# Sigmoid attention with a mixture-of-depths block: picking the routed rows on VectorE instead of on TensorE

## The chip, the cores and the metric

The kernel runs on one core of one Trainium2 chip. A core has five engines that each work through a list of instructions of their own in program order: TensorE (PE, matmuls), VectorE (DVE), ScalarE (ACT), GpSimd (POOL) and SyncE (SP, which here only issues transfers). Data moves between DRAM and the on-chip memory by DMA. The metric is the device time of one execution in microseconds (us); lower is better.

## The reference

Two blocks follow one another. All arrays are float32.

```python
# q, k, v: (8, 12, 448, 64)
scores = scale * np.matmul(q, k.transpose(0, 1, 3, 2)) - np.log(S)
attn = 1.0 / (1.0 + np.exp(-scores))
attn_out = np.matmul(attn, v)
x = attn_out.transpose(0, 2, 1, 3).reshape(8, 448, 768)
# w_gate: (768,), w1: (768, 1024), w2: (1024, 768), capacity: 128
scores = np.einsum('bsd,d->bs', x, w_gate)
out = x.copy()
for b in range(B):
    top_idx = np.argpartition(-scores[b], capacity)[:capacity]
    xe = x[b, top_idx]
    ye = np.maximum(xe @ w1, 0.0) @ w2
    g = 1.0 / (1.0 + np.exp(-scores[b, top_idx]))
    out[b, top_idx] = x[b, top_idx] + g[:, None] * ye
```

So every sequence b has 448 tokens; the 128 with the highest gate score are "routed": they go through a two-layer network, and the others are copied.

## The kernel before

**Steps and pieces.** Four heads of one sequence form a group; there are 24 groups, taken in pairs: 12 *steps* s (`stream`, L463). A step has seven *units* n = 0..6 (`unit`, L193): 32 matmuls make scores into two PSUM tiles named `psc` (of which there are two in all), and two ACT instructions (L220) turn them into `attn`. I write u(s,n) for a unit. Between the units `gap(s, n)` (L445) places other work: in gaps 0 to 2, and in the last gap of the step before, the product with v (`values`, L226, 48 or 64 matmuls into the two PSUM tiles `o`); in gaps 3 to 5 one piece of the routed network (`go`, L406). A gap may take a second piece in n = 5.

**The way of one sequence.** When the last of its three groups has gone through `values`, `take` (L259) transposes the result on DVE into `x_b`, `store` (L280) sends it to a DRAM tile `x_d` by four DMAs on SP, and `gate_part`/`gate` (L269, L290) compute the scores on DVE. `spread` (L300) copies the scores to all partitions with a matmul (L304), ACT makes `rep` of it (L307), and DVE puts each token's own score into `tok_gate` (L309, L313). `rank` (L316), four times, counts for each token the tokens above it, with two DVE instructions each (L321, L324). `place` (L328) adds the counts to a rank and compares it with 0..127 into a matrix of zeros and ones, `sel` (L333). `select` (L336) multiplies this matrix with (token number, score): eight small matmuls (L340) that leave the numbers and the scores of the routed tokens in PSUM, in columns of a `psc` tile that the unit does not use. `fetch` (L343) makes row numbers of them on DVE (L345, L347), the sigmoid of the score on ACT (L349), and an indirect DMA on POOL (L351) gathers the rows as `xe`. `turn_rows` (L356) transposes `xe` with six matmuls (L361). The network then has six pieces for a sequence: three of `ffn1` (L377, 36, 36 and 24 matmuls: g0, g1, g2) and three of `ffn2` (L386, 16 matmuls each: p0, p1, p2), each with an ACT or DVE instruction behind it.

**Where these stand.** `routed(b)` (L421) writes the order out by hand: `late` holds what is placed in gap (s, n), `beside` what is placed inside unit (s, n), between its matmuls and its first ACT instruction. For sequence 0 (called the first sequence; its s is 2): spread in gap (2,5), ranks and place in (2,6), select and fetch inside u(3,1), turn_rows and g0 in (3,3). For sequences 1 to 5 select stands inside u(s+1,0), turn_rows in gap (s+1,3). For sequences 6 and 7 `choose` (L496) places select and fetch behind the last unit. Between the select of sequence 7 and its turn_rows three pieces of sequence 6 are left for PE.

**Loads.** `load(i)` (L90) brings k and q of a group, `turn(i)` (L175) transposes them on DVE; there are two raw buffers of each, so load(i+2) waits for turn(i). `load_v(s+1)` (L100) stands at the start of step s, and its buffer is that of step s-1, read until `values(s-1, 3)` in gap (s,2). `load_weights` (L123) follows it in the steps 1, 2 and 3: five, five and four of the 14 tiles of w1 and w2. All of these, store and `copy_out` (L287) are issued by SP in program order.

Of the kernel before, what the change touches and what calls it, by code (L numbers as in the profile page):

```python
# [17 lines left out]
def kernel(  # L18
# [11 lines left out]
    nc = tc.nc  # L30
# [69 lines left out]
    def load_v(s):  # L100
# [15 lines left out]
        for n in range(4):  # L116
            nc.sync.dma_start(out=th[n * TT:(n + 1) * TT],
                              in_=blocks(4 * (n // 2), HK + n % 2, 4, 1))

    w1_sb = const.tile([P, KD, F], F32, name="w1_sb")  # L120
    w2_sb = const.tile([P, KF, D], F32, name="w2_sb")

    def load_weights(n0, n1):  # L123
        for n in range(max(n0, 0), min(n1, KD + KF)):
            if n < KD:
                nc.sync.dma_start(out=w1_sb[:, n], in_=moe_w1[n * P:(n + 1) * P, :])
            else:
                m = n - KD
                nc.sync.dma_start(out=w2_sb[:, m], in_=moe_w2[m * P:(m + 1) * P, :])
# [6 lines left out]
    wg_b = const.tile([P, HP, TT], F32, name="wg_b")  # L136

    earlier = const.tile([P, NC, S], mybir.dt.uint8, name="earlier")
    iota_r = const.tile([P, CAP], F32, name="iota_r")

    tok_gate = [const.tile([P, NC, 2], F32, name=f"tok_gate{n}") for n in range(2)]
    above = const.tile([P, NC], F32, name="above")
    level = const.tile([P, NC], F32, name="level")
    sel = const.tile([P, NC, CAP], F32, name="sel")

    def constants():
        nc.gpsimd.memset(ones, 1.0)
        make_identity(nc, iden)
        for a in range(4):
            p = slice(a * TT, (a + 1) * TT)  # L150
            nc.gpsimd.dma_start(
                out=wg_b[p],
                in_=bass.AP(tensor=moe_w_gate.tensor, offset=moe_w_gate.offset + a * TT,
                            ap=[[0, TT], [P, HP], [1, TT]]))
        nc.gpsimd.iota(iota_r, pattern=[[1, CAP]], base=0, channel_multiplier=0,
                       allow_small_or_imprecise_dtypes=True)
        for t in (above, level):
            nc.gpsimd.memset(t, 0.0)
        for t in tok_gate:
            nc.gpsimd.memset(t, 0.0)  # L160
            for a in range(4):
                nc.gpsimd.iota(t[a * TT:(a + 1) * TT, :, 0], pattern=[[4, NC]], base=a,
                               channel_multiplier=TB, allow_small_or_imprecise_dtypes=True)
        number = moe.tile([P, TB, TT], F32, name="rep")
        nc.gpsimd.iota(number, pattern=[[1, TB], [TB, TT]], base=0, channel_multiplier=0,
                       allow_small_or_imprecise_dtypes=True)
        for c in range(NC):
            nc.gpsimd.tensor_scalar(
                out=earlier[:, c, :], in0=number.rearrange("p r t -> p (r t)"),
                scalar1=tok_gate[0][:, c, 0:1], scalar2=None, op0=ALU.is_lt)  # L170


    qT, kT, attn, outs = {}, {}, {}, {}
# [19 lines left out]
    def unit(s, n):  # L193


        if (s == 0 and n in (1, 3, 5)) or (s in (1, 2) and n == NF + 1):
            psc = [banks(0), banks(1)]
        else:
            psc = [banks("psc"), banks("psc")]
        if n == NF:  # L200
            parts = [(x, HK) for x in range(2)]
        else:
            x, c = divmod(n, NF + 1)
            parts = [(x, 4 * c), (x, 4 * c + 2)]
        for e in range(2):
            for y, (x, r) in enumerate(parts):
                for h in range(4):
                    d = slice(h * TT, (h + 1) * TT)
                    nc.tensor.matmul(  # L209
                        psc[h // 2][y * Dh:(y + 1) * Dh, h % 2, :S],  # L210
                        kT[2 * s + x][d, e, r:r + 2, :].rearrange("d r t -> d (r t)"),
                        qT[2 * s + x][d, e].rearrange("d r t -> d (r t)"),
                        start=(e == 0), stop=(e == 1))
        more = beside.pop((s, n), [])
        for fn, args in more:
            fn(*args, psc[0][:, 0, S:])
        for pr in range(2):
            a = attnp.tile([P, 2, S], F32, name=f"attn{pr}", bufs=NU + 3)
            attn[s, pr, n] = a
            nc.scalar.activation(a, psc[pr][:, :, :S], AF.Sigmoid, bias=bias_s, scale=QK_SCALE)  # L220
            if pr == 0:
                for fn, args in more:
                    fetch(*args, psc[0][:, 0, S:])

    x_tiles, gate_parts, st = {}, {}, {}
    def values(s, n):  # L226
# [72 lines left out]

    def spread(b, where="o"):  # L300

        tg = tok_gate[b % 2]
        ps = banks(where)[:, 0, :S]
        nc.tensor.matmul(ps, ones, st[b].pop("diag").rearrange("p r t -> p (r t)"),  # L304
                         start=True, stop=True)
        rep = moe.tile([P, S], F32, name="rep")
        nc.scalar.activation(rep, ps, AF.Copy)  # L307
        rep_t = moe.tile([P, TB, TT], F32, name="scr")
        nc.vector.transpose(rep_t, ps.rearrange("p (r t) -> p r t", t=TT))  # L309
        for a in range(4):  # L310
            p = slice(a * TT, (a + 1) * TT)
            n = len(range(a, TB, 4))
            nc.vector.tensor_copy(tg[p, :n, 1], rep_t[p, a:TB:4, 0])  # L313
        st[b]["rep"] = rep

    def rank(b, c):  # L316
        tg, rep = tok_gate[b % 2], st[b]["rep"]
        n = P if c < NC - 1 else LAST
        own = tg[:n, c, 1:2]
        junk = moe.tile([P, S], F32, name="scr")  # L320
        nc.vector.tensor_scalar(out=junk[:n], in0=rep[:n], scalar1=own, scalar2=0.0,  # L321
                                op0=ALU.is_gt, op1=ALU.add, accum_out=above[:n, c:c + 1])
# [3 lines left out]
            op0=ALU.is_equal, op1=ALU.mult, accum_out=level[:n, c:c + 1])  # L326

    def place(b):  # L328
        pl = moe.tile([P, NC], F32, name="place")
        nc.vector.tensor_add(pl, above, level)  # L330
        for c in range(NC):
            n = P if c < NC - 1 else LAST
            nc.vector.tensor_scalar(out=sel[:n, c], in0=iota_r[:n], scalar1=pl[:n, c:c + 1],  # L333
                                    scalar2=None, op0=ALU.is_equal)

    def select(b, s0, n, pk):  # L336

        tg = tok_gate[b % 2]
        for c in range(NC):
            nc.tensor.matmul(pk[:n, 0:2], sel[:, c, s0:s0 + n], tg[:, c, :],  # L340
                             start=(c == 0), stop=(c == NC - 1))

    def fetch(b, s0, n, pk):  # L343
        row = moe.tile([P, 1], I32, name="row", bufs=2)
        nc.vector.tensor_copy(row[:n], pk[:n, 0:1])  # L345
        idx = moe.tile([P, 1], I32, name="idx", bufs=2)
        nc.vector.tensor_scalar_add(idx[:n], pk[:n, 0:1], float(b * S))  # L347
        gt = moe.tile([P, 1], F32, name="gate", bufs=2)
        nc.scalar.activation(gt[:n], pk[:n, 1:2], AF.Sigmoid)  # L349
        xe = moe.tile([P, D], F32, name="xe", bufs=2)  # L350
        nc.gpsimd.indirect_dma_start(  # L351
            out=xe[:n], out_offset=None, in_=st[b]["x_d"][:, :],
# [56 lines left out]
            fn(*args, where)  # L409

    late = {}
    beside = {}

    def put(where, s, n, fn, *args):
        where.setdefault((s, n), []).append((fn, args))
# [5 lines left out]
    def routed(b):  # L421

        s = (NG * b + NG - 1) // 2 + 1
        put(late, s, 5 if b == 0 else 4, spread, b)
        for c in range(NC - 1):
            put(late, s, 6 if b == 0 else 4, rank, b, c)
        put(late, s, 6, rank, b, NC - 1)
        put(late, s, 6, place, b)
        if s == NS:
            return  # L430
        put(late, *((s + 1, 1) if b == 0 else (s, 6)), copy_out, b)
        for s0, n in SLOTS:
            if s + 1 < NS:
                put(beside, s + 1, 1 if b == 0 else 0, select, b, s0, n)
            put(late, s + 1, 3, turn_rows, b, n)
            put(late, s + 1, 3, routed_groups, b, n)

    def gates(i):
        gate_part(i)
# [5 lines left out]
    def gap(s, n):  # L445
# [11 lines left out]
        if n == NU - 1 and s < NS:  # L457
            values(s, 0)
        due(late, s, n)
        if n == 3 and s > 0:  # L460
            gates(2 * s - 1)

    def stream():  # L463
# [1 line left out]
            routed(b)  # L465
        load(0)
        load(1)
        nc.vector.memset(sel, 0.0)
        nc.vector.memset(bias_s, NEG_LOG_S)
        turn(0)  # L470
        load(2)
        load_v(0)
        warm = banks(1)
        for _ in range(3):
            nc.tensor.matmul(warm[:, 0], sel[:, 0, :], sel.rearrange("p c n -> p (c n)"),  # L475
                             start=True, stop=True)
        constants()
        for s in range(NS):
            for n in range(NU):
# [3 lines left out]
                    load(2 * s + 3)  # L483
                if n == 0:
                    load_v(s + 1)
                    load_weights(5 * s - 5, 5 * s)
                if s == 0 and n == 1:
                    nc.vector.tensor_reduce(
                        out=iden_t, in_=iden.rearrange("p (a t) -> p t a", t=TT),
                        axis=AX.X, op=ALU.add)  # L490
                gap(s, n)
                if n == NU - 2:
                    turn(2 * s + 2)
                    load(2 * s + 4)

        def choose(b):  # L496
            for s0, n in SLOTS:
                pk = banks("psc")[:, 0]
                select(b, s0, n, pk)
                fetch(b, s0, n, pk)  # L500

        choose(B - 2)
        for n in range(5):
            gap(NS, n)
        for n in range(3):
            go("any")
        due(late, NS, NU - 1)
        choose(B - 1)
        copy_out(B - 1)
        while len(ready) > 1:  # L510
            go("any")
        for s0, n in SLOTS:
# [1 line left out]
            routed_groups(B - 1, n)  # L514
        while ready:
            go("any")
        assert not late and not beside

    with tc.manual_schedule():
        stream()  # L520
# [29 lines left out]
```

## Time and profile before

| | |
|---|---|
| median of 3 runs | 488.0 us (488.0 to 489.94) |
| the profiled execution | 489.37 us, its span 487.6 us |
| PE busy in the span | 470.9 us (97%) |
| DVE, ACT, POOL busy | 211.7, 189.4 and 28.0 us |
| mean granted TensorE clock | 0.988 |
| DRAM read and written | 53.58 and 25.17 MB |

The span runs from the first to the last instruction of the profiled execution; its time is 1.8 us longer. PE is busy nearly all the time, so a moment in which PE is idle, or a matmul that is not needed, is time of the kernel, while DVE and ACT have room on average. The clock is the share of full TensorE speed that the hardware granted; it is 1.00 in nearly every stretch of this execution.

### The profile page before, as it was taken

To read this page: it belongs to the slowest core of one execution; us is meant where nothing else is said; L and a number is where in the kernel's file an instruction comes from. 1 tells how busy PE (TensorE), PEld (TensorE's weight loads), DVE (VectorE), ACT (ScalarE), POOL (GpSimd) and SP (SyncE) were. 2 spreads that over 40 slices of the span, in tenths; PEclk is the share of its full clock that TensorE was granted. 3 is DMA by queue.
4 is the path that set the end of the run, shared out by engine and by line. 5 is a ranking of instruction groups with operands and counts; after the bars stand their busy time and mean duration, and the time that the engine had idled before them with its cause. 6 is when DMAs were issued, how large, how long until landed. Compare 5 with 4: busy or idle time off the path is not lost.

```text
span 487.6 us, 14593 instructions
## 1 busy us (share of the span) xinstructions
PE 470.9 (97%) x6662; PEld 309.5 (63%) x6662; DVE 211.7 (43%) x461; ACT 189.4 (39%) x253; POOL 28.0 (6%) x45
## 2 busy tenths in 40 slices
PE   8998999499999999999999999999999999999995
PEld 3554646386568465577567476568576667489994
DVE  4315296508252168268152156456433355184101
ACT  4746464223442453544352552543343445011010
POOL 8000000000000000010000000010000000001000
PEclk9999999789999999999999999999999999999999
DMA  8929298985463078498262075658632036165000
GB/s 264 198 83 336 107 311 137 304 249 104 176 152 109 3 166 155 169 221 202 99 153 99 13 173 95 223 131 167 214 82 82 35 59 172 34 97 182 14 34 32
DMA packets 117277, 68.67 MB, mean 141 GB/s; under 512 B 95648, under 2 KB 108000, under 8 KB 116960
## 3 DMA queue, kind: packets, MB, share of 16 engines
q1 hardware_dynamic: 115808, 61.35, 49.0%
q0 software_dynamic: 1408, 6.39, 4.3%
q8 instruction: 52, 0.85, 0.7%
q14 instruction: 9, 0.07, 0.0%
HBM read 53.58 MB, written 25.17 MB: 161 GB/s over the span
## 4 chain that ended last, share of the span: by engine, by line
PE 85%; issue 4%; DMA 3%; DVE 3%; SPq 2%; ACT 1%; POOLq 0%; DVEq 0%; ACTq 0%
PE o L250 24%; PE psc L209 24%; PE o L377 16%; PE o L386 13%; SPq L285 2%; PE o L209 2%; DMA x_d<-x_b 1%; PE psc L386 1%; DMA xe<-x_d,row 1%; PE psc L340 1%; PE o L304 1%; PE o L361 1%; PE o L475 1%; DVE x_b L265 1%; PE psc L377 1%
## 5 line engine op out<-in xcount | busy, mean ns | idle before, releaser
L220 ACT ACTIVATE attn<-psc,bias_s 128x896 f32<-128x896 f32 x158 | 151.1, 1003 | 130.6 <-PE psc L209 117.3
L209 PE MATMUL psc<-qT,kT 32*64 32x448 f32 x2528 | 150.3, 540 | 1.9 <-ACT attn L220 1.9
L250 PE MATMUL o<-attn,raw_v 32*64 32x448 f32 x2304 | 134.7, 536 | 0.7 <-ACT o L253 0.7
L209 PEld LDWEIGHTS psc<-qT,kT 32*64 32x64 f32 x2528 | 61.5, 131 | 61.1 <-issue 37.4
L250 PEld LDWEIGHTS o<-attn,raw_v 32*64 32x64 f32 x2304 | 60.3, 132 | 48.6 <-issue 38.8
L377 PEld LDWEIGHTS o<-xeT,w_sb 128*128 128x128 f32 x672 | 78.9, 197 | 10.7 <-issue 7.9
L377 PE MATMUL o<-xeT,w_sb 128*128 128x128 f32 x672 | 81.7, 282 | 0.9 <-ACT xeT L367 0.9
L386 PE MATMUL o<-w_sb,hT 128*128 128x256 f32 x320 | 73.4, 383 | 0.0
L265 DVE STREAM_TRANSPOSE x_b<-o 128x448 f32<-128x448 f32 x48 | 26.9, 618 | 106.9 <-PE o L250 83.7
L386 PEld LDWEIGHTS o<-w_sb,hT 128*128 128x128 f32 x320 | 59.4, 190 | 16.8 <-issue 5.8
L184 DVE STREAM_TRANSPOSE kT<-raw_k 128x384 f32<-128x384 f32 x48 | 24.7, 554 | 30.2 <-DMA raw_k<-in_k_dram 15.0
L388 DVE SCALAR_TENSOR_TENSOR xe<-o,gate,xe 128x256 f32<-128x256 f32 x20 | 9.7, 483 | 51.5 <-PE o L386 51.5
L379 ACT ACTIVATE hT<-o 128x384 f32<-128x384 f32 (+1 forms) x21 | 9.5, 454 | 56.9 <-PE o L377 56.9
L278 DVE TENSOR_REDUCE gate_p<-scr 128x14 f32<-128x896 f32 x24 | 26.1, 1087 | 0.8
L250 PE MATMUL o<-attn,raw_h 32*64 32x448 f32 x384 | 26.4, 534 | 0.0
L272 DVE TENSOR_TENSOR scr<-x_b,wg_b 128x896 f32<-128x896 f32 x24 | 25.6, 1067 | 0.1
L191 DVE STREAM_TRANSPOSE qT<-raw_q 128x896 f32<-128x896 f32 x23 | 24.7, 1074 | 1.9 <-DMA raw_q<-in_q_dram 1.9
L351 POOL DMA_INDIRECT xe<-x_d,row x8 | 7.9, 987 | 297.0 <-DVE idx L347 222.8
L324 DVE SCALAR_TENSOR_TENSOR scr<-rep,tok_gate,earlier 128x448 f32<-128x448 f32 (+1 forms) x32 | 21.8, 683 | 1.1
L321 DVE TENSOR_SCALAR_CACHE_REDUCE scr<-rep,tok_gate 128x448 f32<-128x448 f32 (+1 forms) x32 | 21.4, 669 | 0.9
L309 DVE STREAM_TRANSPOSE scr<-o 128x448 f32<-128x448 f32 x8 | 5.2, 650 | 37.6 <-ACT rep L307 37.6
L253 ACT ACTIVATE o<-bias_s 1x1 f32<-1x1 f32 x36 | 5.9, 165 | 36.8 <-PE o L250 24.9
(56 smaller groups left out, 204.7 us busy)
## 6 DMA issues: line engine op xcount, KB each, us to landing
raw_k<-in_k_dram SPq DMA_DIRECT2D x24, 448.0 KB, 4.6
raw_q<-in_q_dram SPq DMA_DIRECT2D x24, 448.0 KB, 4.5
x_d<-x_b SPq DMA_DIRECT2D x32, 336.0 KB, 6.7
out_dram<-x_d SPq DMA_DIRECT2D x8, 1344.0 KB, 9.0
raw_v<-in_v_dram SPq DMA_DIRECT2D x48, 192.0 KB, 3.9
w_sb<-in_moe_w_dram SPq DMA_DIRECT2D x6, 512.0 KB, 6.1
w_sb<-in_moe_w_dram SPq DMA_DIRECT2D x8, 384.0 KB, 5.2
raw_h<-in_v_dram SPq DMA_DIRECT2D x48, 32.0 KB, 5.5
```

The source lines that it names most:

```text
L184: nc.vector.transpose(kT[i][:, e, :HK], sk[:, e, :HK].rearrange("p (m c) d -> p c m d", c=NF))
L191: nc.vector.transpose(qT[i], sq)
L209: nc.tensor.matmul(psc[h // 2][y * Dh:(y + 1) * Dh, h % 2, :S], kT[2 * s + x][d, e, r:r + 2, :].rearrange("d r t -> d (r t)"), qT[2 * s + ...
L220: nc.scalar.activation(a, psc[pr][:, :, :S], AF.Sigmoid, bias=bias_s, scale=QK_SCALE)
L250: nc.tensor.matmul(o[x][j * Dh:(j + 1) * Dh, pr, :S], w, a[rows, j, :], start=(n == 0 and c == 0), stop=(n == 3 and c == NF - 1))
L265: nc.vector.transpose(x_tiles[b][:, :, 2 * g + pr, :], outs[s][x][:, pr, :S].rearrange("p (r t) -> p r t", t=TT))
L272: nc.vector.tensor_tensor(out=tmp, in0=x_tiles[b][:, :, 2 * g:2 * g + 2, :].rearrange("p r h d -> p r (h d)"), in1=wg_b[:, 2 * g:2 * g + 2 ...
L278: nc.vector.tensor_reduce(out=gate_parts[b][:, :, g], in_=tmp, axis=AX.X, op=ALU.add)
L321: nc.vector.tensor_scalar(out=junk[:n], in0=rep[:n], scalar1=own, scalar2=0.0, op0=ALU.is_gt, op1=ALU.add, accum_out=above[:n, c:c + 1])
L324: nc.vector.scalar_tensor_tensor(out=junk[:n], in0=rep[:n], scalar=own, in1=earlier[:n, c, :], op0=ALU.is_equal, op1=ALU.mult, accum_out=l ...
L377: nc.tensor.matmul(ps[:, f - f0, :n], w1_sb[:, t, f * P:(f + 1) * P], xeT[:, t, :n], start=(t == 0), stop=(t == KD - 1))
L386: nc.tensor.matmul(ps[:n, :ND], st[b]["hT"][:, t, :n], w2_sb[:, t, cols], start=(t == 0), stop=(t == KF - 1))
```

## The change

The selection matmuls, `sel`, `iota_r` and `beside` go. `place` writes the 448 ranks to a DRAM tile `ranks` by a DMA on SP and reads them back by a second one, broadcast to all partitions (`spot`). `select` compares `spot` with the partition's own number on DVE and sums token numbers (int16) and scores where it is equal: two DVE instructions. It stands in gap (s+1,0) for every sequence but the last. All four ranks and place stand in the gap of spread. The weights are loaded at four points instead of three. For the first sequence turn_rows and g0 move from gap (3,3) to (3,4); in step 2 `turn(6)` and `load(8)` move from n = 5 to n = 3, and the gate of group 3 from n = 3 to n = 6.

```diff
+    WEIGHTS = {(1, 0): (0, 3), (1, NU - 2): (3, 9), (2, 0): (9, 11), (3, 1): (11, KD + KF)}
...
     def place(b):
         pl = moe.tile([P, NC], F32, name="place")
         nc.vector.tensor_add(pl, above, level)
-        for c in range(NC):
-            n = P if c < NC - 1 else LAST
-            nc.vector.tensor_scalar(out=sel[:n, c], in0=iota_r[:n], scalar1=pl[:n, c:c + 1],
-                                    scalar2=None, op0=ALU.is_equal)
-
-    def select(b, s0, n, pk):
-        tg = tok_gate[b % 2]
-        for c in range(NC):
-            nc.tensor.matmul(pk[:n, 0:2], sel[:, c, s0:s0 + n], tg[:, c, :],
-                             start=(c == 0), stop=(c == NC - 1))
-
-    def fetch(b, s0, n, pk):
+        ranks = dram.tile([NC, P], F32, name="ranks")
+        nc.sync.dma_start(out=ranks.rearrange("c p -> p c"), in_=pl)
+        spot = moe.tile([P, S], F32, name="spot")
+        nc.sync.dma_start(out=spot, in_=bass.AP(tensor=ranks.tensor, offset=ranks.offset,
+                                                ap=[[0, P], [1, S]]))
+        st[b]["spot"] = spot
+
+    def select(b, s0, n):
+        picked = []
+        for what in (number.rearrange("p r t -> p (r t)"), st[b]["rep"]):
+            got = moe.tile([P, 1], F32, name="got", bufs=4)
+            junk = moe.tile([P, S], F32, name="scr")
+            nc.vector.scalar_tensor_tensor(
+                out=junk[:n], in0=st[b]["spot"][:n], scalar=slots[s0][:n], in1=what[:n],
+                op0=ALU.is_equal, op1=ALU.mult, accum_out=got[:n, 0:1])
+            picked.append(got)
         row = moe.tile([P, 1], I32, name="row", bufs=2)
-        nc.vector.tensor_copy(row[:n], pk[:n, 0:1])
+        nc.vector.tensor_copy(row[:n], picked[0][:n])
         idx = moe.tile([P, 1], I32, name="idx", bufs=2)
-        nc.vector.tensor_scalar_add(idx[:n], pk[:n, 0:1], float(b * S))
+        nc.vector.tensor_scalar_add(idx[:n], picked[0][:n], float(b * S))
         gt = moe.tile([P, 1], F32, name="gate", bufs=2)
-        nc.scalar.activation(gt[:n], pk[:n, 1:2], AF.Sigmoid)
+        nc.scalar.activation(gt[:n], picked[1][:n], AF.Sigmoid)
...
         put(late, s, 5 if b == 0 else 4, spread, b)
-        for c in range(NC - 1):
-            put(late, s, 6 if b == 0 else 4, rank, b, c)
-        put(late, s, 6, rank, b, NC - 1)
-        put(late, s, 6, place, b)
+        for c in range(NC):
+            put(late, s, 5 if b == 0 else 4, rank, b, c)
+        put(late, s, 5 if b == 0 else 4, place, b)
         if s == NS:
             return
         put(late, *((s + 1, 1) if b == 0 else (s, 6)), copy_out, b)
         for s0, n in SLOTS:
-            if s + 1 < NS:
-                put(beside, s + 1, 1 if b == 0 else 0, select, b, s0, n)
-            put(late, s + 1, 3, turn_rows, b, n)
-            put(late, s + 1, 3, routed_groups, b, n)
+            put(late, s + 1, 0, select, b, s0, n)
+            put(late, s + 1, 4 if b == 0 else 3, turn_rows, b, n)
+            put(late, s + 1, 4 if b == 0 else 3, routed_groups, b, n)
...
-        if n == 3 and s > 0:
+        if n == (NU - 1 if s == 2 else 3) and s > 0:
             gates(2 * s - 1)
...
                 if n == 0:
                     load_v(s + 1)
-                    load_weights(5 * s - 5, 5 * s)
...
                 gap(s, n)
-                if n == NU - 2:
+                if n == (NF if s == 2 else NU - 2):
                     turn(2 * s + 2)
                     load(2 * s + 4)
+                load_weights(*WEIGHTS.get((s, n), (0, 0)))
...
-        choose(B - 2)
         for n in range(5):
             gap(NS, n)
         for n in range(3):
             go("any")
-        due(late, NS, NU - 1)
-        choose(B - 1)
         copy_out(B - 1)
+        for s0, n in SLOTS:
+            select(B - 1, s0, n)
```

Here NU is 7, NF is 3 and NC is 4. The constants change to match: a `slots` tile with the partition's number, `number` with the token numbers as int16 (made on POOL), and `above` starts at 448, so that the 64 unused places of `ranks` equal no slot.

More of the change, by code (lines that the diff above doesn't have):

```diff
@@ L123, in load_weights @@
     def load_weights(n0, n1):
-        for n in range(max(n0, 0), min(n1, KD + KF)):
+        for n in range(n0, n1):
             if n < KD:
@@ L138 @@
     earlier = const.tile([P, NC, S], mybir.dt.uint8, name="earlier")
-    iota_r = const.tile([P, CAP], F32, name="iota_r")
-    tok_gate = [const.tile([P, NC, 2], F32, name=f"tok_gate{n}") for n in range(2)]
+    number = const.tile([P, TB, TT], mybir.dt.int16, name="number")
+    slots = {s0: const.tile([P, 1], F32, name=f"slot{s0}") for s0, _ in SLOTS}
+    score = const.tile([P, NC], F32, name="score")
     above = const.tile([P, NC], F32, name="above")
     level = const.tile([P, NC], F32, name="level")
-    sel = const.tile([P, NC, CAP], F32, name="sel")
     def constants():
@@ L154, in constants @@
                             ap=[[0, TT], [P, HP], [1, TT]]))
-        nc.gpsimd.iota(iota_r, pattern=[[1, CAP]], base=0, channel_multiplier=0,
-                       allow_small_or_imprecise_dtypes=True)
[L157 to L166, printed above, removed]
+        for s0, slot in slots.items():
+            nc.gpsimd.iota(slot, pattern=[[0, 1]], base=s0, channel_multiplier=1,
+                           allow_small_or_imprecise_dtypes=True)
+        nc.gpsimd.memset(above, float(S))
+        nc.gpsimd.memset(level, 0.0)
+        nc.gpsimd.memset(score, 0.0)
+        mine = moe.tile([P, NC], F32, name="place")
+        for a in range(4):
+            nc.gpsimd.iota(mine[a * TT:(a + 1) * TT], pattern=[[4, NC]], base=a,
+                           channel_multiplier=TB, allow_small_or_imprecise_dtypes=True)
+        every = moe.tile([P, TB, TT], F32, name="rep")
+        nc.gpsimd.iota(every, pattern=[[1, TB], [TB, TT]], base=0, channel_multiplier=0,
+                       allow_small_or_imprecise_dtypes=True)
+        nc.gpsimd.tensor_copy(number, every)
         for c in range(NC):
             nc.gpsimd.tensor_scalar(
-                out=earlier[:, c, :], in0=number.rearrange("p r t -> p (r t)"),
-                scalar1=tok_gate[0][:, c, 0:1], scalar2=None, op0=ALU.is_lt)
+                out=earlier[:, c, :], in0=every.rearrange("p r t -> p (r t)"),
+                scalar1=mine[:, c:c + 1], scalar2=None, op0=ALU.is_lt)
     qT, kT, attn, outs = {}, {}, {}, {}
@@ L213, in unit @@
                         start=(e == 0), stop=(e == 1))
-        more = beside.pop((s, n), [])
-        for fn, args in more:
-            fn(*args, psc[0][:, 0, S:])
         for pr in range(2):
@@ L220, in unit @@
             nc.scalar.activation(a, psc[pr][:, :, :S], AF.Sigmoid, bias=bias_s, scale=QK_SCALE)
-            if pr == 0:
-                for fn, args in more:
-                    fetch(*args, psc[0][:, 0, S:])
     x_tiles, gate_parts, st = {}, {}, {}
@@ L312, in spread @@
             n = len(range(a, TB, 4))
-            nc.vector.tensor_copy(tg[p, :n, 1], rep_t[p, a:TB:4, 0])
+            nc.vector.tensor_copy(score[p, :n], rep_t[p, a:TB:4, 0])
         st[b]["rep"] = rep
     def rank(b, c):
-        tg, rep = tok_gate[b % 2], st[b]["rep"]
+        rep = st[b]["rep"]
         n = P if c < NC - 1 else LAST
-        own = tg[:n, c, 1:2]
+        own = score[:n, c:c + 1]
         junk = moe.tile([P, S], F32, name="scr")
@@ L330, in place @@
         nc.vector.tensor_add(pl, above, level)
-        for c in range(NC):
-            n = P if c < NC - 1 else LAST
-            nc.vector.tensor_scalar(out=sel[:n, c], in0=iota_r[:n], scalar1=pl[:n, c:c + 1],
-                                    scalar2=None, op0=ALU.is_equal)
-    def select(b, s0, n, pk):
-        tg = tok_gate[b % 2]
-        for c in range(NC):
-            nc.tensor.matmul(pk[:n, 0:2], sel[:, c, s0:s0 + n], tg[:, c, :],
-                             start=(c == 0), stop=(c == NC - 1))
-    def fetch(b, s0, n, pk):
+        ranks = dram.tile([NC, P], F32, name="ranks")
[13 more added lines that the diff above has]
+            picked.append(got)
         row = moe.tile([P, 1], I32, name="row", bufs=2)
-        nc.vector.tensor_copy(row[:n], pk[:n, 0:1])
+        nc.vector.tensor_copy(row[:n], picked[0][:n])
         idx = moe.tile([P, 1], I32, name="idx", bufs=2)
-        nc.vector.tensor_scalar_add(idx[:n], pk[:n, 0:1], float(b * S))
+        nc.vector.tensor_scalar_add(idx[:n], picked[0][:n], float(b * S))
         gt = moe.tile([P, 1], F32, name="gate", bufs=2)
-        nc.scalar.activation(gt[:n], pk[:n, 1:2], AF.Sigmoid)
+        nc.scalar.activation(gt[:n], picked[1][:n], AF.Sigmoid)
         xe = moe.tile([P, D], F32, name="xe", bufs=2)
@@ L411 @@
     late = {}
-    beside = {}
     def put(where, s, n, fn, *args):
@@ L467, in stream @@
         load(1)
-        nc.vector.memset(sel, 0.0)
+        zero = moe.tile([P, 512], F32, name="scr")
+        nc.vector.memset(zero, 0.0)
         nc.vector.memset(bias_s, NEG_LOG_S)
@@ L474, in stream @@
         for _ in range(3):
-            nc.tensor.matmul(warm[:, 0], sel[:, 0, :], sel.rearrange("p c n -> p (c n)"),
-                             start=True, stop=True)
+            nc.tensor.matmul(warm[:, 0], zero[:, :P], zero, start=True, stop=True)
         constants()
@@ L491, in stream @@
                 gap(s, n)
-                if n == NU - 2:
+                if n == (NF if s == 2 else NU - 2):
                     turn(2 * s + 2)
                     load(2 * s + 4)
[L496 to L500, printed above, removed]
-        choose(B - 2)
+                load_weights(*WEIGHTS.get((s, n), (0, 0)))
         for n in range(5):
@@ L516, in stream @@
             go("any")
-        assert not late and not beside
+        assert not late
     with tc.manual_schedule():
```

## The prediction

> **What bounds the kernel now.** I read the engines' busy times first: PE is busy 470.9 of 487.6 us, so I count what PE is given and where it stands still. The chain of waits confirms it, except in one place, the first routed sequence (its lines: start, length, what):
>
> ```profile
> 78.53 7.14 DMA x_d<-x_b
> 86.54 6.74 DMA xe<-x_d,row
> 93.42 1.53 PE o L361 x6
> 95.83 6.62 PE o L377 x36
> 104.14 4.21 PE o L377 x36
> ```
>
> PE waits for the gathered rows, which wait for the store of x. The windows by stage give PE 2.20 us of work between 87 and 96: 6.8 us idle. The same 36 matmuls take 6.62 us here and 4.21 later, because the granted clock (before "DMA share" in this view) fell:
>
> ```profile
> 94.00:96.00 2.00, 1.10 (x6) 0.70 (x5) 0.00 (x0) 0.81 (x1) 0.00 (x0) 0.50 1.04 382
> 98.00:100.00 2.00, 2.00 (x11) 2.00 (x11) 0.00 (x0) 0.00 (x0) 0.00 (x0) 0.50 1.59 652
> 101.00:102.00 1.00, 1.00 (x12) 1.00 (x11) 0.00 (x0) 0.00 (x0) 0.00 (x0) 1.00 1.58 667
> ```
>
> The stall costs 6.8 + 2.4 = 9.2 us. Next, the timeline of PE at u(6,0), with a select, and at u(5,0), without one:
>
> ```profile
> 193.28 1.71 PE L209 MATMUL psc<-qT,kT 32*64 32x448 f32 x32
> 194.92 1.05 PE L340 MATMUL psc<-tok_gate,sel 128*128 128x2 f32 x8
> 195.91 1.76 PE L250 MATMUL o<-attn,raw_v 32*64 32x448 f32 x32
> 198.96 1.71 PE L209 MATMUL psc<-qT,kT 32*64 32x448 f32 x32
> ...
> 160.68 1.71 PE L209 MATMUL psc<-qT,kT 32*64 32x448 f32 x32
> 165.19 1.71 PE L209 MATMUL psc<-qT,kT 32*64 32x448 f32 x32
> ```
>
> Unit to unit is 5.68 us with, 4.51 without: a select costs PE 1.17 us. Last, SP's own queue around the first store:
>
> ```profile
> 59.87 1.81 SPq L115 DMA_DIRECT2D raw_v<-in_v_dram  x4
> 67.77 13.41 SPq L285 DMA_DIRECT2D x_d<-x_b  x4
> 81.70 2.17 SPq L96 DMA_DIRECT2D raw_k<-in_k_dram  x1
> 83.97 0.37 SPq L96 DMA_DIRECT2D raw_q<-in_q_dram  x1
> ```
>
> The queue stands until `values(1,3)` frees the v buffer (59.87), then issues v, five weights, k, q, and is held by the store for 13.41 us; load(8) follows.
>
> **1. Selects removed from PE.** Sequences 1 to 5: 5 x 1.17 = 5.85 us. Sequence 6: its matmuls start at 415.90, the next ones at 416.89: 1.0. Sequence 7: 0.8 (446.26 to 447.05). Together **-7.65**. Sequence 0's lies inside the stage counted in 2.
>
> **2. The first sequence.** When can `spot` be there? SP: three weights fewer in front (512 + 2 x 384 KB = 1.31 MB). Transfers were saturated there (333 to 392 GB/s between 66 and 74), so the store's data moves 3.5 us forward. In the before trace it ran from 74 to 85, and SP was free at 81.2; after, 70.5 to 81.5 and 77.6. Behind it stands load(8), k and q, 2.6 us: the ranks' write is issued at 80.6. DVE has them by 75.6 (copies end 69.6, four ranks at 1.45, the add 0.16), so the added write waits for SP, not SP for it. Its data waits for k and q (0.92 MB at 390 GB/s, until 83.8) and lands at about 85; the read needs 2.6 us: a 448 KB load on a quiet queue (near 118) lands after 3.2, of which 1.15 are its bytes, and `spot` has 0.55 us of bytes. **Spot at 87.8.** Neither transfer has a row. Bounds: quiet legs of 2.05 and 2.6 without any queueing, 85.3; the gather's 6.7 at this place and raw_h's median of 5.5, 92.8. I take 87.8, built from the rows of this queue.
>
> The page "DMA: Bandwidth & Descriptors" of the Trainium skill (Specifications) speaks against the write: pieces below 512 B are not moved at line rate but by read-modify-write. The nearest row is the store with 2688 pieces of 128 B in 2.70 us, 1.0 ns each; the 512 pieces of 4 B then take 0.5 us, which is in my 85. If the rule doubled that, the sum would be 0.5 us worse here and 0.5 at the end.
>
> What is queued behind it? On DVE, select stands in gap (3,0): two sums at 0.77 (L324's 0.69 and 0.08), then turn(7), 2.4 us. On ACT, the sigmoid of select stands **ahead of the activations of u(3,1)**. Before, that sigmoid waited 0.29 us. Now it waits for spot; u(3,2) needs the psc tiles that those activations read. u(3,2) would start at 80.4. Now: sigmoid at 87.8 + 1.6, first activation done 1.1 later, 90.5, second 91.5. PE stands still for 10 us and runs at half clock after it: in the trace of before the clock fell 3.2 us into the idle time and came back 4.8 us after work went on without a break. From spot on: u(3,2) goes on at +3.7; it and values(2,3), 3.7 us of work, end at +9.9; take 2.3, gate 2.2, gate 2.2 + 0.8 on DVE, +17.4; spread(1), which now stands ahead of g0, +18.3; g0 and, to be level with the trace before, g1: 8.4, **+26.7 = 114.5**. The trace before has the same work done at 109.1 (start of u(3,5)). Loss **+5.4**, which includes the select that is gone. Bounds by those of spot: +2.9 and +10.4. The stall of 87 to 96 does go; a longer one replaces it, 7 us earlier. The gather, issued at 90, has landed by 97 (6.7) and is hidden by u(3,3).
>
> "TensorE: Matmul & The Clock Gate" of the skill (Part 1) gives some 3.4 us of sustained work until full speed. The 4.8 us of this trace disagree. By the page the sum would be 0.7 us lower.
>
> **3. Sequences 1 to 6.** Spot is two quiet legs, 5.2 us, behind the ranks and the store. Tightest is sequence 2: ranks end at 191.4, the store's data at about 193; spot 198, first activation done 200.7. u(6,2) starts at 202.93 - 1.17 = 201.8, and one more piece, 3.65 us, now stands between, as the first sequence's pieces are one gap behind. So 0, with 4.7 us of cover. The same count gives 3 (sequence 1) and about 5 (3, 4, 5). Sequence 6: ranks at 414.5, spot 419.7, gather landed by 427 against turn_rows at 429.4 - 1.0. 0, cover 1.4. DVE does not grow: select's 1.5 us stand against the four compares' 1.1.
>
> **4. The end.** Sequence 7: ranks 442.7, spot 448.2, gather issued 450.1, 5.4 us as before: 455.5. PE is at turn_rows at 456.75 - 0.8 = 455.9. With 0.5 us for the small pieces it just misses: **+0.4** (0 to +6, with 5.5 us a leg).
>
> **5. At nothing.** The four ranks in one gap: between spread and the next use of the `o` tiles PE has 10 us, DVE 9. The constants: POOL is idle from 12.4 on, first need at 70. Weights 3 to 8 at (1,5): transfers at 3 GB/s between 55 and 60, so they fit ahead of v; without that room the store would be 3 us later, and so the stall longer. turn(6), load(8), gate 3: DVE has the room; load(8) ahead of the ranks' write is in 2.
>
> Sum: -7.65 + 5.4 + 0.4 = **-1.85**. From the span of 487.6 that is 485.75, from this execution's 489.37, 487.5; the median is 1.4 us below that execution: **486.1**.
>
> **The rivals.** *Spot comes early.* If the write passed the k and q in front of it and SP were not held by the store, spot could come before 82: then stage 2 breaks even, and at 78 (turn_rows no longer waits) the whole 9.2 + 1.17 come back. For it: DVE is done at 75.6. Against it: 13.41 us of store in SP's queue. Midway: -7.65 - 5 + 0 = **475.4**. Chance 0.26.
>
> *The round trip decides, slower.* Each us more on it costs one us at the first sequence and one at the end, from 3 us on sequence 1 too, from 1.4 sequence 6. It turns the sum past +0.5% at 2.2 us more than mine. With legs of 5.5 (raw_h's median), at 4 us more: -7.65 + 9.4 + 4.4 + 1 + 2.6 = +9.8, **497.8**. For it: the 4 B pieces have no row; against: queues are quiet at the end (30 to 180 GB/s). Chance 0.15.
>
> *It does not do what it says.* The 1.17 us a sequence don't come back, because ACT, with the sigmoid in front, paces the units instead: then 0 in 1, and with 5.4 + 0.4, **493.8**. Against: ACT is busy 189.4 of 487.6. Chance 0.05.
>
> **How the numbers follow.** The forecast has 0.54, its own range 483 to 491. A measurement of this kernel can tell about 0.5% (2.4 us) from nothing: below 485.6 is faster, above 490.4 slower. Of the forecast's 0.54, 0.21 fall below, 0.30 between, 0.03 above. With the early spot faster has 0.47; same 0.30 and a little from the round trip at 1 to 2 us more, 0.32; slower 0.21. The range goes from the early rival's near side to the first us of the late one: 476 to 493.
>
> **What would show it.** L340 gone from PE, and u(s,0) to u(s,1) at 4.5 us throughout. In step 3 PE idle before u(3,2) from about 80, released by ACT, which waits for select; the ranks' write issued near 80.6 and spot near 88; half clock until about 97. No idle PE in the later steps, and less than 1 us before the last turn_rows. Wrong: an unbroken PE between 80 and 92 (early rival), or idle PE ahead of u(s+1,2) in several steps (late rival).

## The result and the profile after

The changed kernel takes 543.4 us (four executions, 540.9 to 543.7) against 488.5 for the kernel before: a ratio of 1.111, 95% interval 1.107 to 1.115. The forecast was 486.1, its range 476 to 493. The span of the profiled execution grew from 487.6 to 541.6 us. These lines of the page after (engines; the clock granted, in tenths over 40 slices; the groups of instructions) answer to those of before:

```profile
span 541.6 us, 14483 instructions
...
PE 481.4 (89%) x6598; PEld 312.1 (58%) x6598; DVE 215.9 (40%) x461; ACT 189.1 (35%) x253; POOL 27.7 (5%) x41
...
PEclk9999996799899999999999999899999999699799
...
L214 PE MATMUL psc<-qT,kT 32*64 32x448 f32 x2528 | 164.9, 554 | 35.7 <-ACT attn L222 34.0
...
L343 DVE SCALAR_TENSOR_TENSOR scr<-spot,slot,number 128x448 f32<-128x448 f32 x8 | 5.5, 685 | 112.5 <-DMA spot<-ranks 112.5
...
L352 ACT ACTIVATE gate<-got 128x1 f32<-128x1 f32 x8 | 1.6, 203 | 67.4 <-DVE scr L343 67.4
```

PE was idle 16.7 us before and is idle 60.2 now, and although 64 matmuls are gone (8.3 us busy before) it is busy 10.5 us longer, in part because the clock falls in the long waits. The windows by stage around four of the waits (the clock stands before the last two columns, DMA share and GB/s) show it below 1.00 in three of them, and at 1.00 in a shorter one, near 388:

```profile
78.00:98.80 20.80, 3.29 (x72) 1.68 (x56) 2.73 (x11) 1.18 (x3) 0.86 (x1) 0.68 0.34 79
137.00:146.60 9.60, 2.51 (x58) 0.95 (x43) 2.63 (x10) 1.22 (x3) 0.91 (x1) 0.85 0.69 215
...
386.00:391.00 5.00, 2.50 (x46) 1.44 (x35) 2.77 (x10) 1.34 (x3) 0.57 (x1) 1.00 0.97 399
457.00:466.00 9.00, 1.75 (x21) 0.74 (x25) 1.51 (x6) 0.37 (x2) 0.00 (x0) 0.73 0.60 178
```

The score matmuls (L214) waited 34.0 us for ACT; the first instruction of select (L343) waited 112.5 us for `spot`, and the sigmoid behind it on ACT (L352) 67.4 us for select. The chain is plain in the kernel's step s = 3. First SP's queue, with start and length of each issue:

```profile
81.86 0.39 SPq L331 DMA_DIRECT2D ranks<-place  x1
...
93.09 0.33 SPq L333 DMA_DIRECT2D spot<-ranks  x1
```

The read can be issued only when the write has landed: 11.2 us. Then DVE, ACT and PE, each a timeline (start, length, engine, line; in brackets the idle time before it and what ended it):

```profile
96.16 0.69 DVE L343 SCALAR_TENSOR_TENSOR scr<-spot,slot,number 128x448 f32<-128x448 f32 x1 [18.04 <-DMA spot<-ranks]
```

```profile
97.62 0.20 ACT L352 ACTIVATE gate<-got 128x1 f32<-128x1 f32 x1 [19.82 <-DVE scr L343]
...
97.73 1.89 ACT L222 ACTIVATE attn<-psc,bias_s 128x896 f32<-128x896 f32 x2
```

```profile
78.80 2.46 PE L249 MATMUL o<-attn,raw_v 32*64 32x448 f32 x46
98.77 3.43 PE L214 MATMUL psc<-qT,kT 32*64 32x448 f32 x26 [17.51 <-ACT attn L222]
```

The sigmoid of select stands ahead of the activations of u(3,1); u(3,2) needs the psc tiles that they read. So a transfer of 2 KB stops PE for 17.5 us, by way of three engines (SP, DVE and ACT). The same happens at each later sequence: 7.1 us at sequence 1, 1.6 to 2.5 at 2, 4 and 5, 0.5 at 3, 7.0 at 6, 7.5 at 7. And the DMA engines were not busy meanwhile. The windows after the ranks' write of sequence 6, which was issued at 449.41:

```profile
450.00:451.00 1.00, 0.67 (x16) 0.00 (x0) 0.00 (x0) 0.16 (x1) 0.00 (x0) 1.00 0.32 18
451.00:452.00 1.00, 0.94 (x24) 0.55 (x32) 0.00 (x0) 0.01 (x1) 0.00 (x0) 1.00 0.03 0
...
457.00:458.00 1.00, 0.72 (x9) 0.41 (x9) 0.00 (x0) 0.00 (x0) 0.00 (x0) 1.00 0.00 0
```

Its packets are over by 452; it lands at 457.9. Sequence 2, whose write meets a quiet queue too, shows both legs, the write and the read:

```profile
209.29 0.39 SPq L331 DMA_DIRECT2D ranks<-place  x1
217.61 0.33 SPq L333 DMA_DIRECT2D spot<-ranks  x1
```

```profile
223.85 0.68 DVE L343 SCALAR_TENSOR_TENSOR scr<-spot,slot,number 128x448 f32<-128x448 f32 x1 [11.12 <-DMA spot<-ranks]
```

The write takes 8.3 us and the read 6.2. From the issue of the write to select it is 14.2 to 15.8 us at every sequence, quiet queue or not; my sum had 5.2 for a quiet queue and 7.2 for the first sequence.

### The profile page after: what moved, and what is told of

Same layout as the page of the kernel before. It is cut to its first block, busy times and chain, and to the rows that moved or that the text cites. A ratio compares the mean times of both kernels' runs of the same rounds, so it can differ in the third digit from the quotient of the medians.

```text
span 541.6 us, 14483 instructions
## 1 busy us (share of the span) xinstructions
PE 481.4 (89%) x6598; PEld 312.1 (58%) x6598; DVE 215.9 (40%) x461; ACT 189.1 (35%) x253; POOL 27.7 (5%) x41
## 5 line engine op out<-in xcount | busy, mean ns | idle before, releaser
L214 PE MATMUL psc<-qT,kT 32*64 32x448 f32 x2528 | 164.9, 554 | 35.7 <-ACT attn L222 34.0
L249 PE MATMUL o<-attn,raw_v 32*64 32x448 f32 x2304 | 149.4, 549 | 8.4 <-ACT o L252 7.7
L214 PEld LDWEIGHTS psc<-qT,kT 32*64 32x64 f32 x2528 | 65.5, 134 | 103.1 <-ACT attn L222 53.8
L249 PEld LDWEIGHTS o<-attn,raw_v 32*64 32x64 f32 x2304 | 69.8, 135 | 60.2 <-issue 42.2
L380 PEld LDWEIGHTS o<-xeT,w_sb 128*128 128x128 f32 x672 | 76.7, 192 | 9.1 <-issue 6.7
L380 PE MATMUL o<-xeT,w_sb 128*128 128x128 f32 x672 | 79.1, 277 | 0.0
L343 DVE SCALAR_TENSOR_TENSOR scr<-spot,slot,number 128x448 f32<-128x448 f32 x8 | 5.5, 685 | 112.5 <-DMA spot<-ranks 112.5
L189 DVE STREAM_TRANSPOSE kT<-raw_k 128x384 f32<-128x384 f32 x48 | 24.7, 553 | 21.7 <-DMA raw_k<-in_k_dram 7.6
L249 PE MATMUL o<-attn,raw_h 32*64 32x448 f32 x384 | 28.5, 535 | 0.0
L352 ACT ACTIVATE gate<-got 128x1 f32<-128x1 f32 x8 | 1.6, 203 | 67.4 <-DVE scr L343 67.4
L389 PE MATMUL psc<-w_sb,hT 128*128 128x256 f32 x64 | 16.2, 407 | 7.5 <-ACT hT L382 7.5
L322 DVE SCALAR_TENSOR_TENSOR scr<-rep,score,earlier 128x448 f32<-128x448 f32 (+1 forms) x32 | 21.9, 683 | 1.1
```

The source lines that it names most:

```text
L189: nc.vector.transpose(kT[i][:, e, :HK], sk[:, e, :HK].rearrange("p (m c) d -> p c m d", c=NF))
L214: nc.tensor.matmul(psc[h // 2][y * Dh:(y + 1) * Dh, h % 2, :S], kT[2 * s + x][d, e, r:r + 2, :].rearrange("d r t -> d (r t)"), qT[2 * s + ...
L249: nc.tensor.matmul(o[x][j * Dh:(j + 1) * Dh, pr, :S], w, a[rows, j, :], start=(n == 0 and c == 0), stop=(n == 3 and c == NF - 1))
L322: nc.vector.scalar_tensor_tensor(out=junk[:n], in0=rep[:n], scalar=own, in1=earlier[:n, c, :], op0=ALU.is_equal, op1=ALU.mult, accum_out=l ...
L380: nc.tensor.matmul(ps[:, f - f0, :n], w1_sb[:, t, f * P:(f + 1) * P], xeT[:, t, :n], start=(t == 0), stop=(t == KD - 1))
L389: nc.tensor.matmul(ps[:n, :ND], st[b]["hT"][:, t, :n], w2_sb[:, t, cols], start=(t == 0), stop=(t == KF - 1))
```

## The experiments

Theory A: the loss is the round trip through DRAM, waited for in program order by DVE and ACT, and what makes it long is the write in 4-byte pieces. The rivals are named in the expectations.

**The ranks in pieces of 128 bytes.**

```diff
...
-        pl = moe.tile([P, NC], F32, name="place")
-        nc.vector.tensor_add(pl, above, level)
+        nc.vector.tensor_add(wide[:, :NC], above, level)
+        pl = moe.tile([P, TT], F32, name="placeT")
+        nc.vector.transpose(pl, wide)
         ranks = dram.tile([NC, P], F32, name="ranks")
-        nc.sync.dma_start(out=ranks.rearrange("c p -> p c"), in_=pl)
+        for a in range(4):
+            nc.sync.dma_start(out=ranks[:, a * TT:(a + 1) * TT], in_=pl[a * TT:a * TT + NC, :])
```

> The changed kernel, but the ranks are turned by one more DVE transpose and written to DRAM in 16 pieces of 128 bytes (four DMAs) instead of 512 pieces of 4 bytes. Theory A (the loss is the round trip, and most of the round trip is the landing of a write in 4-byte pieces): the write lands in 2.5 to 4.5 us instead of 8.1 to 10.3, the idle PE ahead of u(s+1,2) goes for sequences 2 to 5 and shrinks by about 5 us for 0, 1, 6 and 7: 505 to 520 us. Rival B (any write that is read back takes that long, whatever its pieces): the write still lands after 8 us, 540 to 548 us.

Measured: 492.0 us, ratio 1.0035 (1.0006 to 1.0064). Better than theory A had it: 51.6 of the span's 54 us are gone with this one edit. SP's queue for sequence 2, and PE at u(3,2):

```profile
195.17 1.29 SPq L335 DMA_DIRECT2D ranks<-placeT  x4
197.47 0.34 SPq L337 DMA_DIRECT2D spot<-ranks  x1
```

```profile
91.79 3.43 PE L216 MATMUL psc<-qT,kT 32*64 32x448 f32 x26 [10.13 <-ACT attn L224]
```

From the first of the four writes to the read it is 2.3 us, where it was 8.3. PE does not wait for it at sequences 2 to 7 any more, and for 0.3 us at sequence 1. What is left is the first sequence: 10.1 us idle at u(3,2). Rival B falls.

**The sigmoid later.** The activation of `gt` is taken out of select and put first in `turn_rows`.

```diff
-        gt = moe.tile([P, 1], F32, name="gate", bufs=2)
-        nc.scalar.activation(gt[:n], picked[1][:n], AF.Sigmoid)
...
     def turn_rows(b, n, where="o"):
+        gt = moe.tile([P, 1], F32, name="gate", bufs=2)
+        nc.scalar.activation(gt[:n], st[b]["score"][:n], AF.Sigmoid)
...
```

> The changed kernel, but the sigmoid of the routed scores on ACT is issued just ahead of turn_rows instead of in select; the round trip stays as slow as it is. Theory A (ACT, in program order behind that sigmoid, is what holds the psc tiles and so PE): no idle PE ahead of u(s+1,2) for sequences 1 to 5, the waits at sequences 6 and 7 fall, 510 to 522 us; what stays is the first sequence, where turn(7) is behind select on DVE: PE then waits ahead of u(3,3). Rival C (DVE, where the transposes stand behind select, is what holds PE): the idle time only moves from u(s+1,2) to u(s+1,3), 535 us or more.

Measured: 526.6 us, ratio 1.073 (1.066 to 1.079): between theory A (510 to 522) and rival C (535 or more). PE's waits (who waited for what: us in total, times, longest):

```profile
PE psc L214 <- DVE qT L196: 15.6, 1, 15.6
PE psc L365 <- DMA xe<-x_d,row: 8.4, 1, 8.4
PE o L365 <- DVE xe L392: 4.6, 1, 4.6
...
PE psc L214 <- ACT attn L222: 2.9, 3, 1.4
```

ACT's hold was real: 34.0 us of waits fell to 2.9, and the time by 17 us. But the long trip then showed through DVE at the first sequence, where turn(7) stands behind select (15.6 us), and through the gathered rows (8.4 us; L365 is the transposing matmul of turn_rows). Theory A was right in what goes and too low in what stays.

**No round trip.** `spot` is a constant tile; the first 128 tokens of each sequence are routed.

```diff
-        ranks = dram.tile([NC, P], F32, name="ranks")
-        nc.sync.dma_start(out=ranks.rearrange("c p -> p c"), in_=pl)
-        spot = moe.tile([P, S], F32, name="spot")
-        nc.sync.dma_start(out=spot, in_=bass.AP(tensor=ranks.tensor, offset=ranks.offset,
-                                                ap=[[0, P], [1, S]]))
-        st[b]["spot"] = spot
+        st[b]["spot"] = fixed
```

> The changed kernel without the round trip: spot is a constant tile 0, 1, 2, ..., so the first 128 tokens of every sequence are routed, not those with the highest scores; everything else stays, the ranks are still computed. Theory A (the round trip is the whole loss): all idle PE released by ACT behind select goes, PE gets back 1.17 us a sequence and most of the stall of the first: 470 to 477 us. Rival D (the matmuls' 1.17 us a sequence don't come back, as something else paces PE): 479 to 484 us. If more than the round trip costs: above 490 us.

Measured: 476.8 us, ratio 0.974 (0.968 to 0.979), as theory A had it. The trip is the whole loss.

**The moves alone.** The kernel before, with its matmul selection, and the new places of weights, turn(6), load(8), gates and the first sequence's pieces.

```diff
...
-                    load_weights(5 * s - 5, 5 * s)
...
-                if n == NU - 2:
+                if n == (NF if s == 2 else NU - 2):
                     turn(2 * s + 2)
                     load(2 * s + 4)
+                load_weights(*WEIGHTS.get((s, n), (0, 0)))
...
-            put(late, s + 1, 3, turn_rows, b, n)
-            put(late, s + 1, 3, routed_groups, b, n)
+            put(late, s + 1, 4 if b == 0 else 3, turn_rows, b, n)
+            put(late, s + 1, 4 if b == 0 else 3, routed_groups, b, n)
```

> The kernel before, with its selection by matmuls, but with the other half of the change: weights at four points, turn(6), load(8) and the gate of group 3 moved, the first sequence's ranks in gap (2,5) and its turn_rows in (3,4), all ranks and place in one gap. Theory A: the store of the first sequence ends 2.6 us earlier, the gathered rows are there when PE comes to turn_rows one unit later, idle PE there falls from 6.8 to under 2 us and the clock stays up: 478 to 483 us. Rival E (the stall only moves, or the moved pieces make another wait): 486 to 490 us.

Measured: 483.1 us, ratio 0.986 (0.982 to 0.991), at the upper edge of theory A. PE around the first turn_rows (L362), where it had been idle for 6.8 us:

```profile
89.84 2.65 PE L210 MATMUL psc<-qT,kT 32*64 32x448 f32 x32 [1.14 <-ACT attn L221]
92.42 0.87 PE L362 MATMUL o<-iden,xe 128*128 128x128 f32 x6
94.84 1.02 PE L305 MATMUL o<-rep,ones 128*128 128x448 f32 x2 [1.54 <-DVE rep L295]
95.69 4.18 PE L378 MATMUL o<-xeT,w_sb 128*128 128x128 f32 x36
```

PE no longer waits for the gathered rows, and the first piece takes 4.18 us, at full clock, instead of 6.62. Rival E falls. The spans of the profiled executions now split the change:

| step | span, us | difference |
|---|---|---|
| kernel before | 487.6 | |
| + the moves | 481.7 | -5.9 |
| + select on DVE, no trip (first 128 tokens) | 474.5 | -7.2 |
| + the trip, 128-byte pieces | 490.0 | +15.5 |
| + the trip, 4-byte pieces (the change) | 541.6 | +51.6 |

Each span is of one execution; the medians of all executions give -6.6, -6.3, +15.2 and +51.4.

**Why the write is slow, measured by itself.** Pieces of 128 bytes changed three things: their size, their number, and the transpose with four DMAs. Eight forms of write were put behind the last work of the kernel before.

```diff
...
+        forms = [("a", [NC, P], lambda d: (d.rearrange("c p -> p c"), src[:, :NC])),
+                 ("b", [P, NC], lambda d: (d, src[:, :NC])),
+                 ("c", [P, NC, 16], lambda d: (d[:, :, 0], src[:, :NC])),
+                 ("d", [P, NC, 128], lambda d: (d[:, :, 0], src[:, :NC])),
+                 ("e", [1, P], lambda d: (d.rearrange("c p -> p c"), src[:, :1])),
...
```

> The kernel before, with eight small writes to DRAM added behind its last work, twice over, each followed by a read of one element of what was written; the read's issue shows when the write has landed. a: 512 pieces of 4 bytes, neighbours in DRAM, as the ranks; b: 128 pieces of 16 bytes; c: 512 of 4 bytes, 64 bytes apart; d: 512 of 4 bytes, 512 bytes apart; e: 128 of 4 bytes, neighbours; f: 128 of 64 bytes; g: 128 of 128 bytes; h: 16 of 128 bytes. Theory A (a piece under some size lands late, wherever it lies): a, c, d and e land in about 8 us, g and h in 1.5 to 2.5, b and f between. Rival F (pieces that share a line of DRAM wait for one another): a and e near 8, d near 2. Rival G (it is the number of pieces): a, c and d near 8, e near 3.

Measured in one execution, the second time through, the forms a to e, from SP's queue (the issue of `back` shows that the write ahead of it has landed):

```profile
513.67 0.39 SPq L532 DMA_DIRECT2D dst_a<-src  x1
521.76 0.21 SPq L534 DMA_DIRECT2D back<-dst_a  x1
522.02 0.34 SPq L532 DMA_DIRECT2D dst_b<-src  x1
524.70 0.21 SPq L534 DMA_DIRECT2D back<-dst_b  x1
524.96 0.52 SPq L532 DMA_DIRECT2D dst_c<-src  x1
527.66 0.21 SPq L534 DMA_DIRECT2D back<-dst_c  x1
527.92 0.52 SPq L532 DMA_DIRECT2D dst_d<-src  x1
530.23 0.21 SPq L534 DMA_DIRECT2D back<-dst_d  x1
530.49 0.34 SPq L532 DMA_DIRECT2D dst_e<-src  x1
537.63 0.21 SPq L534 DMA_DIRECT2D back<-dst_e  x1
```

The ranks' form (a) lands in 8.1 us (10.5 the first time). The same 512 pieces of 4 bytes, 64 bytes apart (c), land in 2.7, 512 bytes apart (d) in 2.3. A quarter as many, next to each other (e), still need 7.1. So my part of theory A on the size of a piece falls, and so does rival G: neither the size nor the number alone makes a write late. What rival F forecast is what came, whether or not a shared line of DRAM is the reason: 4-byte pieces are late when pieces of many partitions are neighbours in DRAM. Among neighbours the size does matter: 16 bytes (b) took 2.7 us, and 1.4 the first time, 64 bytes (f) 2.8, 128 bytes (g and h) 1.5 and 1.4.

**The same inside the kernel, without transpose or further DMAs.** The ranks stand in another order, and the first 128 tokens are routed.

```diff
-        ranks = dram.tile([NC, P], F32, name="ranks")
-        nc.sync.dma_start(out=ranks.rearrange("c p -> p c"), in_=pl)
+        ranks = dram.tile([P, NC], F32, name="ranks")
+        nc.sync.dma_start(out=ranks, in_=pl)
...
-        nc.vector.tensor_copy(row[:n], picked[0][:n])
+        nc.vector.tensor_copy(row[:n], slots[s0][:n])
...
```

> The changed kernel with one edit to the write: the ranks are written by the one DMA in 128 pieces of 16 bytes, a partition's four next to each other, instead of 512 pieces of 4 bytes; no transpose, no further DMAs. They then stand in another order in DRAM than token numbers and scores, so the picked numbers are not the routed tokens; the row numbers are copied from the slot tile instead, at the same place in DVE's order, and the first 128 tokens of every sequence are routed with scores that are not theirs. Theory F (the write is late because 4-byte pieces of many partitions share a line of DRAM; 16-byte pieces landed in 1.4 to 2.7 us by themselves): the write lands in 1.4 to 3 us where the queue is quiet, and the kernel takes 489 to 494 us, like the one with 128-byte pieces. If it was the transpose or the four queued DMAs that helped there: above 520 us.

Measured: 491.1 us, ratio 1.001 (0.9985 to 1.0044), the time of the 128-byte pieces. Sequences 2 and 3 in SP's queue:

```profile
195.72 0.34 SPq L331 DMA_DIRECT2D ranks<-place  x1
197.13 0.33 SPq L333 DMA_DIRECT2D spot<-ranks  x1
...
234.24 0.34 SPq L331 DMA_DIRECT2D ranks<-place  x1
236.98 0.33 SPq L333 DMA_DIRECT2D spot<-ranks  x1
```

1.4 and 2.7 us, as by itself. It is the layout of one DMA's destination, 4-byte words of all partitions side by side, that cost some 52 us of the span (541.6 against 489.6).

**What is left of the first sequence.** Both edits, short pieces and the sigmoid later:

> The changed kernel with both edits: ranks in pieces of 128 bytes, and the sigmoid of the routed scores just ahead of turn_rows. Theory A (with the short trip only the first sequence is late, held by ACT first and DVE second): PE no longer waits ahead of u(3,2), but ahead of u(3,3) for turn(7), which stands behind select on DVE, some 5 to 7 us: 485 to 488 us. Rival H (DVE and the clock cost nothing there): 478 to 481 us.

Measured: 487.7 us, ratio 0.995 (0.992 to 0.997), within theory A; the wait ahead of u(3,3) for the transposes was 8.5 us, longer than expected. Then the first sequence's select in gap (3,2) and its turn_rows in (3,5); and, in a second kernel, load(8) issued behind the ranks:

```diff
-            put(late, s + 1, 0, select, b, s0, n)
-            put(late, s + 1, 4 if b == 0 else 3, turn_rows, b, n)
-            put(late, s + 1, 4 if b == 0 else 3, routed_groups, b, n)
+            put(late, s + 1, 2 if b == 0 else 0, select, b, s0, n)
+            put(late, s + 1, 5 if b == 0 else 3, turn_rows, b, n)
+            put(late, s + 1, 5 if b == 0 else 3, routed_groups, b, n)
```

> Both edits, and the first sequence's select moved to gap (3,2), behind the take and one gate part on DVE, its turn_rows to gap (3,5); the others stay. Theory A (nothing but the wait for spot in program order is left to gain): no idle PE over 1 us ahead of u(3,2) or u(3,3), 2 to 5 us ahead of spread(1), 476 to 480 us, below both kernels and the moves alone (483).

> As f1, with load(8) on SP behind the first sequence's ranks instead of ahead of them. Theory A: spot comes about 3 us earlier, at 85 to 87, select no longer waits, 475 to 479 us; at most 2 us below f1.

The first kernel (f1 in the expectation of the second) measured 486.2 us (ratio 0.992, 0.989 to 0.995). It misses, and its waits say where:

```profile
PE o L304 <- DVE rep L295: 5.9, 2, 5.1
...
PE psc L216 <- ACT attn L224: 3.0, 3, 1.4
...
PE o L369 <- DMA xe<-x_d,row: 1.6, 1, 1.6
```

The units no longer wait, but spread(1) does, 5.1 us: its scores come from DVE, where two gate parts now stand behind take and select, and PE stands behind spread in program order. I had allowed 2 to 5 us for it and nothing for the clock, which fell again (0.89 between 80 and 125 us). Moving select moved the wait. For the second kernel the expectation was, once more:

> As f1, with load(8) on SP behind the first sequence's ranks instead of ahead of them. Theory A: spot comes about 3 us earlier, at 85 to 87, select no longer waits, 475 to 479 us; at most 2 us below f1.

It measured 485.4 us (ratio 0.991, 0.988 to 0.995). The read of `spot` was issued 4.3 us earlier (82.40 against 86.68) and select did not wait, as expected, but the time misses: spread(1) still waited, 3.9 us. Its executions lie between 482 and 488; why so far apart is open.

**A mixture.** So the first sequence keeps its matmuls, and the others, whose trip is hidden, go through DRAM in 128-byte pieces. `pick` is select without the sigmoid, which stands in turn_rows; sel shares its buffer with spot.

```diff
     def place(b):
+        if b > 0:
+            nc.vector.tensor_add(wide[:, :NC], above, level)
+            pl = moe.tile([P, TT], F32, name="placeT")
+            nc.vector.transpose(pl, wide)
...
-            if s + 1 < NS:
-                put(beside, s + 1, 1 if b == 0 else 0, select, b, s0, n)
+            if b == 0:
+                put(beside, s + 1, 1, select, b, s0, n)
+            else:
+                put(late, s + 1, 0, pick, b, s0, n)
```

> The moves alone (483 us), with the selection by matmuls kept for the first sequence, and for the others the broadcast through DRAM in pieces of 128 bytes, select on DVE in gap (s+1,0) and the sigmoid ahead of turn_rows. Theory A (the broadcast costs nothing where the trip is short and hidden, and takes some 0.9 us a sequence from PE): six of the selects go, 476 to 479 us, 3 us at most above the version without any trip. If the later trips are not hidden: 481 us or more.

Measured: 479.5 us against 490.4, ratio 0.977 (0.975 to 0.980): just above theory A, and faster than both kernels and than the moves alone. Seven selects go, not six as I wrote. DVE waits in it too,

```profile
DVE scr L384 <- DMA spot<-ranks: 37.4, 7, 11.4
...
PE psc L219 <- ACT attn L230: 3.0, 3, 1.4
```

but none of these 37.4 us reaches PE's score matmuls: their 3.0 us are there in the moves alone, too.

## Why the prediction was wrong

**Step 2, the term that failed: "Its data waits for k and q ... and lands at about 85."** The write was issued at 81.9 (I had 80.6) and landed at 93.1: 11.2 us, where I had 4.4. I priced 512 pieces of 4 bytes by the store's 1.0 ns for each piece of 128, and put the read-modify-write rule of the Trainium skill ("DMA: Bandwidth & Descriptors", Specifications) at 0.5 us more here and at the end. Piece size alone was the wrong question: measured by itself, the same write with its words 512 bytes apart landed in 2.3 us. At sequence 6 the write's packets were over in some 2 us, and what took 6 more was the landing of words that are neighbours in DRAM. For other pieces my 4.4 was right: at the same place, behind the same k and q, 128-byte pieces landed after 4.5 us and 16-byte pieces after 4.7. My upper bound, the gather's 6.7 us, was a price for a busy queue, not for this; 11.2 lay outside both ends.

**The rest of step 2 held.** I had PE idle for 10 us ahead of u(3,2), held by ACT behind the sigmoid; with 128-byte pieces it was 10.1. From spot to u(3,5) I had 22.5 us (26.7 less one piece); it was 21.7 in the changed kernel (96.16 to 117.83) and 22.5 with 128-byte pieces (89.18 to 111.72). With the short write, spot came 1.4 us after my 87.8. So step 2 describes the kernel with that other write. The whole forecast would have been 6 us too low for it (492.0 against 486.1), though inside its range; spot's 1.4 us and step 1 are part of that, and the rest I have not traced.

**Step 1 was too large.** "A select costs PE 1.17 us" gave 8.8 us with the first sequence's; the moves alone and the version without a trip are 7.2 apart by the spans and 6.3 by the medians, 0.8 to 0.9 each. Why is not settled.

**Step 3: "0" with covers of 1.4 to 5 us.** The trip outgrew the covers: at sequence 2 I had 2.6 us for the write and 2.6 for the read, and it took 8.3 and 6.2. The read's share I had not seen: it is 5.4 to 6.2 us at sequences 1 to 6, and 3.3 to 4.7 with 128-byte pieces; why it is longer behind the slow write is not shown. Nine us more than reckoned leave 6.1, 4.4, 4, 4, 4 and 7.7 us at sequences 1 to 6; measured were 7.1, 1.6, 0.5, 1.9, 2.5 and 7.0. So the covers at 2 to 5 were larger than I counted. At sequence 6 the agreement is luck: I had counted the gather against turn_rows, and PE waited before that, in `values`, for an ACT instruction behind the sigmoid. The clock I had priced at the first sequence alone; it fell at 1, 4, 6 and 7 as well. PE's busy time rose by 18.8 us over what the removed matmuls leave. The busy time in windows of lower clock, times the clock that was missing, is 11 us in the profiled execution of the changed kernel and 3 in that of the kernel before, so the clock explains some 8 of the 18.8. Most of the rest lies around the waits of sequences 2 to 5, mostly at a clock of 1.00, and is open.

**Step 4: "it just misses".** By its own numbers (455.5 + 0.5 against 455.9) the miss was 0.1 us and not 0.4. With the short trip the last turn_rows waits for nothing; with the long one ACT's sigmoid held the first `ffn2` piece of sequence 6 for 7.5 us, through hT, which I did not have.

**Step 5 and the moves.** Costing them at nothing was right, and they earn 5.9 us by themselves, which I had let the new stall swallow.

**The rivals.** The round trip decided, as the second one said, and beyond its price: I gave it 4 us more and 497.8, it was 9 more and 543.4, for which its own slopes, an added 1 us at the first sequence and at the end and the covers of step 3 between them, give 534. (With the slope of sequence 6 it passes +0.5% at 1.9 us more, not at 2.2.) It had a chance of 0.15. The early spot did not come; that the selects' time doesn't come back is refuted by the version without a trip, where most of it does.

## What to carry to other kernels

A small transfer that is written and read back on the way of in-order engines is priced by when it lands, not by its bytes or packets; where no row shows its shape, its bound must be open upwards, or it must be measured by itself. Before a kernel writes a column of words from many partitions to DRAM, turn it so that each piece is 16 bytes or more, or keep the words apart (64 bytes were enough here). And an instruction that waits for such a transfer should stand on each engine only as early as its result is needed.

## What the runs showed of the hardware

- A write of 4-byte words from 128 partitions to neighbouring addresses in DRAM landed after 8.1 to 11.2 us in the changed kernel and 7.1 to 10.5 by itself, with the DMA engines idle for most of it where the queue was quiet; with words 64 bytes apart it took 2.7 to 2.95, 512 bytes apart 2.3. Sixteen-byte neighbours took 1.4 to 2.7. What makes neighbours wait, and over what length, was not tried.
- In the changed kernel the clock fell to 0.50 in each of PE's four waits of 7 us and more, 2.4 to 4.3 us after PE went idle, and came back 3.9 to 5.6 us after work resumed. Of the shorter waits it fell after one of 1.9 us (sequence 4, for 3.4 us) and not after one of 2.5 (sequence 5).
